# Folded weight loaded and split in the last turns, a new fixed order, and other places for chunk 6's copies

## The chip, the cores and the metric

One core of one Trainium2 chip runs the kernel. The metric is device time in microseconds of one execution, the median of several runs. TensorE (PE) does the matrix products, VectorE (DVE), ScalarE (ACT) and GpSimd (POOL) the elementwise work, and SyncE (SP) issues the transfers.

## What is computed

```python
def reference(**kwargs):            # attention, then two MLPs
    attn_out = _attn_ref(q, k, v)   # 4 x 8 heads, 576 positions, 64 wide; window masks
    x = attn_out.transpose(0, 2, 1, 3).reshape(2304, 512)
    x = _moe_ref(x, w_in, w_out)
    return _moe2_ref(x, w1, w2, w3, w_out)

def _moe_ref(x, w_in, w_out):       # 512 -> 2048 -> 512
    h = x @ w_in
    g = np.maximum(0.01 * h, h)
    return g @ w_out

def _moe2_ref(x, w1, w2, w3, w_out):   # 512 -> 1024 -> 512
    a = x @ w1
    b = x @ w2
    h = a * b @ w3
    return h @ w_out
```

Everything is float32, some of the inputs arrive as 64-bit words that the kernel converts.

## The kernel before

A float32 product is made of three matmuls on a high and a low part of each operand (`mm3`, lines 132 to 134). The two parts come from `split_steps`: a cast to the high part (L122) and a subtraction for the low one (L124), each on an engine named by the caller. So a third of TensorE's matmuls stand on each of the lines 132, 133 and 134, whatever they compute; tiles tell them apart.

The program has two halves. The first is written out by hand: the string `START` has one letter for each step of each stage, `LOADS` one letter for each load (a letter `L` in `START` takes the next one), and the instructions stand in each engine's queue in that order. It holds the attention (`ps_s`, `ps_p`, `ps_o`), the first MLP, the fold of `w3 @ w_out` of the second MLP into one weight, and the preparation of the second MLP's weights.

- The first MLP works on 7 chunks of tokens. For a chunk there are 16 turns, 112 in all: a turn makes `ps_h` (12 matmuls), its activation `g` (L545), the two parts `gs` of `g`, and adds 12 matmuls of 384 columns to the chunk's sums `ps_x`. At the end of a chunk `evacuate_steps` copies `ps_x` into `st` (L621) and stores it.
- The fold writes the product of `w3` and the last weight to memory (`wp_dram`); `w3` is transposed on TensorE (`ps_w3T`) after its conversion (`wf`).
- The weights of the second MLP are combined into seven sums per block (`weight_sums`, tiles `sum` and `ws`), and parts of the result y of the first MLP into seven sums (`sum_y_steps`: `ysum`, `ys`).

The second half is left to the scheduler. For each of 3 pairs of token chunks (p) and 8 blocks (i), `gate` makes seven products of six matmuls each into tiles `ps_m`: products 0 and 1 share a pair of banks, 2 and 3 another pair, both from two buffers called "acc"; 4, 5 and 6 have a bank each. ScalarE copies three of them (`e1`, `e2`, `e5`, L783), VectorE adds them up (`c21`, `c11`, `c22`, L787), and the gated result is split into `p` on ScalarE and GpSimd. The accumulators `ps_x` of the chunks use the two "acc" buffers too, so that the first gate must wait until they have been copied. Behind the eight gates of a p, `final` multiplies `p` by the folded weight (`ps_y`).

The folded weight is fetched in the gates of p = 0: `load_wp` loads 128 of its 1024 rows into a staging tile `wpf` (two buffers), and `split_wp` splits them on ScalarE and GpSimd into `wps`, a tile that takes over the place of an eighth of the first MLP's `w_out` (tag "wo"). Chunk 6's copies `st` take a tile of the tag "o", which has two places, where the four copies of a chunk need four.

Who splits what is set by letters in tables: A is ScalarE, D is VectorE, G is GpSimd.

Of the kernel before, what the change touches and what calls it, by code (L numbers as in the profile page):

```python
# [28 lines left out]
def tile_window_attention_two_mlps(  # L29
# [801 lines left out]
    with ExitStack():  # L831
# [71 lines left out]
        START = (
            "L~L~~~~LTL~Y~~LT~Y~~SLTMXSYLqTMXLE~~~Y~wqEwSRNTMLRPXNCSYLqEwPMTCLLXVYRqVx~NyxTEySYwL"
            "RLTMNLXPLY~CqEwSGDPMLVALRXCSNLxBL~MqEwPUVyGSLXxLARq~y~C~M~NEXVBDGwPqEwLx~R~~GN~y~C~R"
            "DANPVCDIBPUxOVLCy~IxVUAHOxGyyBIAGHLUgBODILcHgUAlIOcDgJlBOGLUcHDAlIGFBHgLAUcBHOglLIDL"
            "HGgOAUGHDgIAGDBJOALUBDGIJLUBLOILUcHAGOIlBJOALGgcBDlHZAGgUzHcADlBDUJgBDUIJcOIlGIJUcgO"
            "AIJDBlcGOJlAcDGUHBlDIOLAJULgOBIHUGOIDGAHOcBDLGAUJglBIgDJLcOAlGcUHBZLAIDzHOgBUGIcHlgA"
            "OlBGJDgLAUDBUJFLJULcLIclLISOISMlHGOMXAFqEwJGXLBOHgRAGNcBDHlqEwUDPUgJIRDgNCIcOHAlGOBD"
            "GHALUgLFAVIgJOxLBycDLBUHlIUOIJcgGlAOJBDGcULAlHIDcOBlGHgUADIHBOgULJgIO|FPJCcLlSclSMHX"  # L910
            "MqEwFVHXLgxqyJgRENwRPcFJCNlPZcHClzVgFVxLJyxyJclLLJcLlSSMXHMqEwXJqgRcHENwlPgRHcCNlPgJ"
            "CVclVxyJxGyADHBULHIOgclJgGHcADlBHgULIOHgSgSMGXJADqMBHEXLUqEwwIOHZRzNJcRlgGPJCcNADlBJ"
            "cglLUPcIOHClHgGADHgBULJIOJclgGJcADlBJclLUJcIOlHGHgDAclBHgULIOJgVclLVxHyGxyADJBgULJcF"
            "IOlJLclHLHgclHgHgFHgLSSMJFXLJcqMXlEJcqwgRlEJcNwRlFHNHgZLczlHgFJgLHclPgHCFSSMLJMXXqEw"
            "PcJlFCJqEwcLRlNJgcRlJcNFVlVxLHyxyJgclPHCSgclSMXHMqXPgEHqCwERVgNwVxLJRxyNyPclJCLSclSM"
            "FJMLFHXJgLXqcqEPwHlCRENwVgcVRxlyHxLNyFPgHCLPgJCFVVxcJLxylLyHclHgHgSSMXHMqEwXqJRENJwc"
            "RlJcNgPZlHCczlgSgSMFHXLMqJXFEJqwLcRElwPNgHCRcNlVFgVxJLxyyPcHClFSgSMJXMqEwXqPcHCRlEwN"
            "VgRNVxHyxLyPHCSSMJXMqXqEPcJCwlERgwNVRVcxNHyxlygPJCPcHClgVV^LLLLLLLprprprxJ0yxy01d1dJ"
            "c2l2L3gLJ3cl4cH5l601dWg2Wp3Lr4pL405Jr1dL5626WLc3lWp0rWpd1Lr42LW50L31Jd62p3LWrpLr4WL5"
            "061dHe2f3LpHgrpcLrJglLWclWp4rp40JL5r106L5d16W2d32LHp3LrHLgclWgWpr4LWp05r1HdL623L4gW0"  # L920
            "p5dr1W6pL2rH3LLef4J50p61dr2WcLlLJ3pgrLWicjlkWpmr4J50Lp61dr2HcLlL3WgWpr4pLW05r16LH2d3"
            "L4gW0p5dr1W6pL2rHeL3f4W50p61dWrpL2rW3L4W56JprpL4cWr5l6LWgHprpWrW!JeLLfLJcLlgJcalboJc"
            "hlLnHaHgobclhJgnL78Jc9$la%bHo&h*nLJg+ac-blH=oh<nLHg7ac8lb9Jgoh$nLJca%lb&Hho*nL+Jg-c="
            "lH<a78oHg9bclhHgnL$a%Jogb&*hJ+cLnlHc-l=Hg<a78obJ9gh$nJLca%lbHihocj&LHgn*k+mlH-g=<Ha7"
            "obJ8h9n$LJca%ob&Jhcl*LnglJcg+l-Hc=l<Hg7a8ob9H$h%gnLJ&a*ob+Jch-lL=Jcgnl<Hca7l8bo9Hgh$"
            "nHg%a&boJ*h+nHc-l=gJ<789J$c%l&Jgc*l+Jc-l=H<@sHgtclvJgssJctlvtJvssJ#tvtivjksmtvstv"
        )
# [174 lines left out]
```

## Time and profile before

| what | us |
|---|---|
| median of 3 runs | 842.15 (841.25 to 842.74) |
| the profiled execution | 842.99 |
| its span, first to last instruction | 840.8 |
| TensorE's matmuls busy | 823.4 |
| VectorE, ScalarE, GpSimd busy | 507.6, 378.8, 221.2 |

The span is measured by the profiler from the first to the last instruction of the core; 2.2 us of the execution's own time lie around it. Busy time is the time in which an engine has an instruction in work, added up over the span. TensorE's granted clock is at its higher level from 20 us on. The rest of the profile is read below in single rows.

### The profile page before, as it was taken

What the parts mean: (1) busy time and instruction counts of PE and PEld (TensorE: products, weight loads), DVE (VectorE), ACT (ScalarE), POOL (GpSimd) and SP (SyncE); (2) the same over time, 40 slices, a digit from 0 to 9 for tenths busy, and PEclk for the clock granted to TensorE, in tenths of its full rate; (3) what the DMA queues carried; (4) which work ended last, traced back from release to release, by engine and by line L of the source; (5) the groups of instructions that cost most, each with busy time, mean ns of one, the idle gap of its engine ahead of it and who ended that gap; (6) DMA issues with size and microseconds to landing.
All of it is one profiled execution on the core that took longest, in us unless ns stands there. A gap on an engine that the chain in (4) does not pass through costs nothing.

```text
span 840.8 us, 15523 instructions
## 1 busy us (share of the span) xinstructions
PE 823.4 (98%) x5818; PEld 780.1 (93%) x5818; DVE 507.6 (60%) x1001; ACT 378.8 (45%) x831; POOL 221.2 (26%) x252
## 2 busy tenths in 40 slices
PE   7999999999999999999999999989999999999998
PEld 7899999999999999899889999979988999889987
DVE  3999986444647364565545667776792277606730
ACT  3999873442233333556545665443341234213311
POOL 3514422343334334321203200025211022102210
PEclk9999999999999999999999999999999999999999
DMA  6996855445454432465638787668755377426001
GB/s 134 266 322 185 240 151 160 119 138 146 120 148 112 96 93 84 147 206 174 224 114 276 267 277 245 238 218 313 240 189 205 101 262 239 132 69 225 14 26 51
DMA packets 104570, 146.37 MB, mean 174 GB/s; under 512 B 44720, under 2 KB 70064, under 8 KB 104496
## 3 DMA queue, kind: packets, MB, share of 16 engines
q1 hardware_dynamic: 104496, 145.39, 56.2%
q8 instruction: 46, 0.75, 0.4%
q14 instruction: 28, 0.23, 0.1%
HBM read 115.87 MB, written 29.49 MB: 173 GB/s over the span
## 4 chain that ended last, share of the span: by engine, by line
PE 85%; DVE 5%; ACT 3%; DMA 3%; issue 2%; POOL 1%; SPq 0%; ACTq 0%; DVEq 0%; POOLq 0%
PE ps_h L132 7%; PE ps_x L132 7%; PE ps_h L134 7%; PE ps_x L133 7%; PE ps_h L133 7%; PE ps_x L134 7%; PE ps_m L132 7%; PE ps_m L134 7%; PE ps_m L133 7%; PE ps_y L132 4%; PE ps_y L133 4%; PE ps_y L134 4%; PE ps_s L408 3%; PE ps_o L494 2%; PE ps_p L473 2%
## 5 line engine op out<-in xcount | busy, mean ns | idle before, releaser
L132 PE MATMUL ps_h<-x,win 128*128 128x384 f32 (+2 forms) x448 | 143.0, 319 | 0.7 <-DVE win L124 0.7
L134 PE MATMUL ps_h<-x,win 128*128 128x384 f32 (+2 forms) x448 | 140.0, 312 | 0.0
L133 PE MATMUL ps_h<-x,win 128*128 128x384 f32 (+2 forms) x448 | 139.9, 312 | 0.0
L132 PE MATMUL ps_m<-ys,ws 128*128 128x384 f32 x336 | 114.1, 341 | 6.7 <-ACT e L783 6.0
L132 PE MATMUL ps_x<-gs,wout 128*128 128x384 f32 (+2 forms) x356 | 114.7, 322 | 0.2 <-ACT st L621 0.2
L133 PE MATMUL ps_m<-ys,ws 128*128 128x384 f32 x336 | 113.3, 337 | 0.0
L134 PE MATMUL ps_x<-gs,wout 128*128 128x384 f32 (+2 forms) x356 | 112.4, 316 | 0.0
L133 PE MATMUL ps_x<-gs,wout 128*128 128x384 f32 (+2 forms) x356 | 112.4, 316 | 0.0
L134 PE MATMUL ps_m<-ys,ws 128*128 128x384 f32 x336 | 111.2, 337 | 0.0
L124 POOL TENSOR_TENSOR gs<-g,gs 128x384 fp32r<-128x384 f32 (+2 forms) x70 | 65.9, 944 | 151.7 <-DVE gs L122 136.0
L124 POOL TENSOR_TENSOR p<-c,p 128x384 fp32r<-128x384 f32 x48 | 49.4, 1048 | 190.7 <-ACT p L122 185.5
L545 ACT ACTIVATE g<-ps_h 128x384 f32<-128x384 f32 (+2 forms) x112 | 49.3, 441 | 102.0 <-PE ps_h L134 73.9
L132 PEld LDWEIGHTS ps_h<-x,win 128*128 128x128 f32 x448 | 84.5, 189 | 3.0 <-issue 0.9
L133 PEld LDWEIGHTS ps_h<-x,win 128*128 128x128 f32 x448 | 84.6, 189 | 0.3
L134 PEld LDWEIGHTS ps_h<-x,win 128*128 128x128 f32 x448 | 84.5, 189 | 0.0
L787 DVE TENSOR_TENSOR c<-c,ps_m 128x384 f32<-128x384 f32 x96 | 49.7, 549 | 52.4 <-PE ps_m L134 40.6
L132 PEld LDWEIGHTS ps_m<-ys,ws 128*128 128x128 f32 x336 | 63.0, 188 | 10.6 <-ACT e L783 8.8
L783 ACT COPY e<-ps_m 128x384 f32<-128x384 f32 x72 | 34.1, 480 | 77.3 <-PE ps_m L134 46.6
L132 PEld LDWEIGHTS ps_x<-gs,wout 128*128 128x128 f32 x356 | 67.1, 189 | 1.8 <-ACT st L621 0.5
L122 DVE CAST gs<-g 128x384 fp32r<-128x384 f32 (+2 forms) x84 | 32.0, 383 | 60.2 <-PE ps_x L134 44.1
L133 PEld LDWEIGHTS ps_x<-gs,wout 128*128 128x128 f32 x356 | 67.2, 189 | 0.2
L134 PEld LDWEIGHTS ps_x<-gs,wout 128*128 128x128 f32 x356 | 67.1, 189 | 0.0
(131 smaller groups left out, 1731.0 us busy)
## 6 DMA issues: line engine op xcount, KB each, us to landing
ws<-ws_dram SPq DMA_DIRECT2D x63, 512.0 KB
raw<-in_moe_w_out_dram SPq DMA_DIRECT2D x24, 512.0 KB
ws_dram<-ws SPq DMA_DIRECT2D x24, 512.0 KB
raw<-in_moe_w_in_dram SPq DMA_DIRECT2D x16, 512.0 KB
rawf<-in_moe_w_dram SPq DMA_DIRECT2D x16, 512.0 KB
wo2f<-wo_dram SPq DMA_DIRECT2D x32, 256.0 KB
rawl<-in_moe_w_dram SPq DMA_DIRECT2D x16, 512.0 KB
q<-in_q_dram SPq DMA_DIRECT2D x48, 140.0 KB
```

The lines of the kernel that those rows point to most:

```text
L122: copy_on(e_hi)(hi, src)
L124: e_lo.tensor_tensor(lo, src, hi.bitcast(F32), op=ALU.subtract)
L132: nc.tensor.matmul(ps, a[1], b[0], start=first, stop=False)
L133: nc.tensor.matmul(ps, a[0], b[1], start=False, stop=False)
L134: nc.tensor.matmul(ps, a[0], b[0], start=False, stop=last)
L408: nc.tensor.matmul(ps[j * QB : (j + 1) * QB, i - bl.start], qt[d, i * QB : (i + 1) * QB], kt[d, first_key(i, plain) : first_key(i, plain) ...
L473: nc.tensor.transpose(pss[g][:, i - i0], s[:, i], ident)
L494: nc.tensor.matmul(ps[j * D : (j + 1) * D, i * QB : (i + 1) * QB], vt[i][:, h + j, :], t[:, i, j * QB : (j + 1) * QB], start=True, stop=True,)
L545: nc.scalar.activation(g, ps, AF.Prelu, alpha=SLOPE)
L783: nc.scalar.copy(t, a)
L787: e.tensor_tensor(t, a, b, op=op)
```

## The change

The edits:

1. The folded weight is loaded and split within the last 12 turns of `START`. `LOADS` has eight new letters `t`, `START` eight pairs `,` and `;`, for a new stage `split_wp`. The load goes straight into the low half of the place in `wo`, there is no staging tile, and the subtraction is done on VectorE in place. Each load waits for chunk 6's last matmul on the eighth of `w_out` whose place it takes.
2. Chunk 6's four copies go into two tiles of the tag "p", which has sixteen places (the results' own).
3. `e5`, `c21` and `c11` have two buffers each in the gates, like `e1` and `e2` before.
4. `START`, `LOADS` and the tables that name engines are other ones. Of the tables, in counts: the high part of the 16 turns' `gs` in the later chunks (entry `1`) goes from VectorE to ScalarE; 14 heads, not 18, take their exponentials in one instruction.

```diff
     GS_ON = {
-        0: "DG", 1: "DD",
+        0: "DG", 1: "AD",
...
                         if c == NCH - 1:
-                            st = fin.tile([P, DM], F32, tag="o", name=f"st{c}_{i}_{j}", bufs=2)[:, :n]
+                            if j == 0:
+                                st6 = fin.tile([P, 2, MT], F32, tag="p", name=f"st{c}_{i}", bufs=2 * NI)
+                            st = st6[:, j]
...
     def load_wp(ib):
-        t = fin.tile([P, DM], F32, tag="wpf", name=f"wpf{ib}", bufs=2)
-        nc.sync.dma_start(t, wp_dram[ib * P : (ib + 1) * P, :])
-        wsum[ib] = t
+        wp[ib] = wo_slot(f"wps{ib}")
+        nc.sync.dma_start(wp[ib][:, 1].bitcast(F32), wp_dram[ib * P : (ib + 1) * P, :])
 
     def split_wp(ib):
-        t = wo_slot(f"wps{ib}")
-        split(t[:, 0], t[:, 1], wsum.pop(ib), nc.scalar, nc.gpsimd)
-        wp[ib] = t
+        t = wp[ib]
+        yield from split_steps(t[:, 0], t[:, 1], t[:, 1].bitcast(F32), nc.scalar, nc.vector)
...
-        TWICE = ("e1", "e2")
+        TWICE = ("e1", "e2", "e5", "c21", "c11")
...
-            "lH<a78oHg9bclhHgnL$a%Jogb&*hJ+cLnlHc-l=Hg<a78obJ9gh$nJLca%lbHihocj&LHgn*k+mlH-g=<Ha7"
+            "ohH$nLm%aJ&bo*h+JLcnL-lJcLgl=g<HcL7al8ob9H$h%gnLJ,&a;*obJL+,-c;hJLl=Lng,<cHL;alc7blH"
...
+            ",;": split_wp,
...
+                    elif y == "t":
+                        load_wp(len(wp))
...
                 gate(p, i)
-                if p == 0:
-                    load_wp(i)
-                    split_wp(i)
```

How the change moves instructions is shown at three places. In the names below, the number behind the last underscore is a serial number of the tile.

*ScalarE's queue at the passage from the last turn into the gates.* Before, with the copies `st6`, the casts of `wps` and the copies `e10_0` and `e20_0` of the first gate:

```order
551 L621 COPY st6_0_1_6691<-ps_x6_0_0_6180 128x384
552 L122 CAST wps0_6793<-wpf0_6791 128x512
553 L783 COPY e10_0_6720<-ps_m0_0_0_6719 128x384
554 L122 CAST wps1_6878<-wpf1_6876 128x512
555 L621 COPY st6_1_1_6699<-ps_x6_0_1_6181 128x384
556 L783 COPY e20_0_6728<-ps_m0_0_0_6719 128x384
557 L122 CAST ys0_5_6702<-ysum0_5_6697 128x768
558 L122 CAST wps2_6967<-wpf2_6965 128x512
559 L122 CAST wps3_7052<-wpf3_7050 128x512
560 L783 COPY e10_1_6805<-ps_m0_1_0_6804 128x384
561 L783 COPY e50_0_6755<-ps_m0_0_2_6736 128x384
```

The same place in the changed kernel:

```order
575 L122 CAST ys0_4_6722<-yf0_5596 128x768
576 L122 CAST ys0_5_6727<-ysum0_5_6724 128x768
577 L623 COPY st6_0_6729<-ps_x6_0_0_6199 128x384
578 L623 COPY st6_1_6735<-ps_x6_0_1_6200 128x384
579 L783 COPY e10_0_6755<-ps_m0_0_0_6754 128x384
580 L122 CAST ys0_6_6742<-ysum0_6_6738 128x768
581 L783 COPY e20_0_6763<-ps_m0_0_0_6754 128x384
582 L783 COPY e50_0_6790<-ps_m0_0_2_6771 128x384
583 L783 COPY e10_1_6835<-ps_m0_1_0_6834 128x384
584 L783 COPY e20_1_6843<-ps_m0_1_0_6834 128x384
```

The casts of `wps` are gone from between the copies, and the cast of `ys0_5` stands ahead of the copies `st6`.

*TensorE's queue in gate 4 of p = 0.* Before, with the end of the second product (`ps_m0_4_0` from `ys0_1`) and the beginning of the third (`ps_m0_4_2`):

```order
3230 L132 MATMUL ps_m0_4_0_7063<-ys0_1_6642,ws0_4_1_6798 128x384
3231 L133 MATMUL ps_m0_4_0_7063<-ys0_1_6642,ws0_4_1_6798 128x384
3232 L134 MATMUL ps_m0_4_0_7063<-ys0_1_6642,ws0_4_1_6798 128x384
3233 L132 MATMUL ps_m0_4_2_7080<-ys0_2_6646,ws0_4_2_6800 128x384
3234 L133 MATMUL ps_m0_4_2_7080<-ys0_2_6646,ws0_4_2_6800 128x384
```

In the changed kernel the third product of that gate stands ahead of the second, which follows here:

```order
3239 L134 MATMUL ps_m0_4_2_7095<-ys0_3_6688,ws0_4_1_6828 128x384
3240 L132 MATMUL ps_m0_4_4_7117<-ys0_4_6722,ws0_4_2_6830 128x384
...
3249 L132 MATMUL ps_m0_5_6_7215<-ys0_6_6742,ws0_5_3_6916 128x384
3250 L132 MATMUL ps_m0_4_0_7078<-ys0_1_6651,ws0_4_1_6828 128x384
3251 L133 MATMUL ps_m0_4_0_7078<-ys0_1_6651,ws0_4_1_6828 128x384
3252 L134 MATMUL ps_m0_4_0_7078<-ys0_1_6651,ws0_4_1_6828 128x384
```

Where the third product followed the second at once, ten matmuls of other products and the second one now stand behind the third.

*ScalarE's queue in chunk 6, from the activation of `ps_h6_8` to that of `ps_h6_9`.* Before (`lw` and `rl` are the conversion of weights):

```order
519 L545 ACTIVATE g_85<-ps_h6_8_6285 128x384
520 L117 ACTIVATE lw12_6301<-rawl13_6242 128x512
521 L122 CAST ws0_0_2_6348<-sum0_2_6344 128x2x256
522 L163 ACTIVATE rl13_6346<-rawl13_6242 128x512
523 L165 ACTIVATE rl13_6346<-rawl13_6242 128x512
524 L122 CAST ws0_0_3_6373<-sum0_3_6368 128x2x256
525 L545 ACTIVATE g_85<-ps_h6_9_6310 128x384
```

In the changed kernel, the first twelve of what stands there:

```order
534 L545 ACTIVATE g_85<-ps_h6_8_6293 128x384
535 L122 CAST wps2_6279<-wps2_6279 128x512
536 L122 CAST gs_1825<-g_85 128x384
537 L117 ACTIVATE lw14_6400<-rawl14_6313 128x512
538 L122 CAST gs_1825<-g_85 128x384
539 L163 ACTIVATE rl14_6401<-rawl14_6313 128x512
540 L122 CAST ws0_1_0_6423<-sum1_0_6405 128x256
541 L165 ACTIVATE rl14_6401<-rawl14_6313 128x512
542 L122 CAST ws0_1_1_6428<-lw12_6283 128x2x256
543 L122 CAST wps3_6349<-wps3_6349 128x512
544 L117 ACTIVATE lw14_6400<-rawl15_6376 128x512
545 L122 CAST wps4_6371<-wps4_6371 128x512
```

Three more follow (two `rl`, one `ws`) before the `g` of `ps_h6_9`: three casts of `wps`, two of `gs` and a second conversion have come in between the two activations.

## Rows read from the trace of the kernel before

**Rows 1.** The page: busy time by engine, and the chain that ended last.

```profile
PE 823.4 (98%) x5818; PEld 780.1 (93%) x5818; DVE 507.6 (60%) x1001; ACT 378.8 (45%) x831; POOL 221.2 (26%) x252
...
PE 85%; DVE 5%; ACT 3%; DMA 3%; issue 2%; POOL 1%; SPq 0%; ACTq 0%; DVEq 0%; POOLq 0%
```

**Rows 2.** TensorE's waits, 552 us to the end, then before: total, times, longest.

```profile
PE ps_m L132 <- ACT e L783: 6.0, 8, 1.4
PE ps_m L132 <- ACT st L621: 0.7, 2, 0.4
...
PE ps_w3T L665 <- DVE wf L169: 0.8, 1, 0.8
...
PE ps_h L132 <- DVE win L124: 0.7, 1, 0.7
```

**Rows 3.** Timeline of TensorE: start, duration, instruction, in brackets the idle time before.

```profile
554.50 0.34 PE L134 MATMUL ps_m<-ys,ws 128*128 128x384 f32 x1
555.95 0.44 PE L132 MATMUL ps_m<-ys,ws 128*128 128x384 f32 x1 [1.12 <-ACT e L783]
556.23 0.34 PE L133 MATMUL ps_m<-ys,ws 128*128 128x384 f32 x1
...
613.53 0.45 PE L132 MATMUL ps_m<-ys,ws 128*128 128x384 f32 x1 [0.62 <-ACT e L783]
```

**Rows 4.** Timeline of ScalarE at the passage.

```profile
554.90 0.62 ACT L122 CAST wps<-wpf 128x512 fp32r<-128x512 f32 x1 [2.32 <-DMA wpf<-wp_dram]
555.42 0.47 ACT L783 COPY e<-ps_m 128x384 f32<-128x384 f32 x1
```

**Rows 5.** The chain that ended last, 552 to 564 us: start, duration, what.

```profile
552.99 3.30 DMA x_dram<-st
...
558.36 4.06 DMA wpf<-wp_dram
...
562.45 0.62 ACT wps L122
```

**Rows 6.** VectorE: one row of its timeline, and of its waits from 552 to 640 us.

```profile
556.41 0.56 DVE L621 COPY st<-ps_x 128x384 f32<-128x384 f32 x1 [3.72 <-DMA x_dram<-st]
...
DVE c L787 <- POOL p L124: 9.6, 12, 1.3
```

**Rows 7.** A stretch of the windows: length, busy time (instructions) by engine, clock, DMA.

```profile
640.00:660.00 20.00, 20.00 (x92) 16.82 (x91) 0.56 (x1) 2.28 (x4) 1.01 (x1) 1.00 0.27 85
```

**Rows 8.** The instructions on the tile `wpf`: duration in ns, least, median, most.

```profile
L122 ACT CAST wps<-wpf x8: 617/620/627, 554.9 to 579.6; 128x512 fp32r<-128x512 f32 x8
L124 POOL TENSOR_TENSOR wps<-wpf,wps x8: 1281/1285/1296, 555.6 to 582.1; 128x512 fp32r<-128x512 f32 x8
```

**Rows 9.** VectorE by form, 477 to 640 us: busy, mean ns, idle time before.

```profile
L124 DVE TENSOR_TENSOR gs<-g,gs 128x384 fp32r<-128x384 f32 x16 | 8.9, 554 | 0.1
L124 DVE TENSOR_TENSOR ws<-sum,ws 128x512 fp32r<-128x512 f32 x12 | 8.3, 690 | 4.5 <-ACT ws L122 4.5
...
L122 DVE CAST gs<-g 128x384 fp32r<-128x384 f32 x17 | 6.1, 359 | 7.2 <-PE ps_x L134 4.5 <-ACT g L545 1.5 <-POOL gs L124 0.9
...
L748 DVE TENSOR_TENSOR ysum<-yf 128x768 f32<-128x768 f32 x4 | 3.8, 953 | 0.0
```

**Rows 10.** The sum of five windows of 15 us, 477 to 552 us (chunk 6).

```profile
sum 75.00, PE 75.00 PEld 74.92 DVE 54.35 ACT 42.20 POOL 1.73; mean PE 15.00 PEld 14.98 DVE 10.87 ACT 8.44 POOL 0.35
```

**Rows 11.** Timeline of TensorE at the first transposed block of `w3`.

```profile
346.95 0.34 PE L134 MATMUL ps_x<-gs,wout 128*128 128x384 f32 x1
348.10 0.66 PE L665 MATMUL ps_w3T<-ident,wf 128*128 128x128 f32 x4 [0.81 <-DVE wf L169]
```

**Rows 12.** The sum of five windows of 20 us, 20 to 120 us.

```profile
sum 100.00, PE 98.06 PEld 93.17 DVE 93.31 ACT 90.26 POOL 38.47; mean PE 19.61 PEld 18.63 DVE 18.66 ACT 18.05 POOL 7.69
```

**Rows 13.** The instructions on the tile `yf`, 555 to 580 us: ns, first and last start.

```profile
L748 DVE TENSOR_TENSOR ysum<-yf,yf x3: 1397/1603/2054, 556.9 to 572.5; 128x768 f32<-128x768 f32 x3
L741 SPq DMA_DIRECT2D yf<-x_dram x2: 371/433/495, 563.3 to 563.7; - x2
```

More of the change, by code (lines that the diff above doesn't have):

```diff
@@ L177, in tile_window_attention_two_mlps @@
     FOLD_CONV = ("GAD",)
-    P_ON = "ADDAAAAAAAAADDADAAAAAAAAAAAAAAAA"
-    X_ON = "AADADADDADADDADDAAAAAAAAAAAAAAAA"
-    ONE_EXP = (0, 3, 6, 11, 13, 14, 16, 17, 20, 21, 22, 23, 25, 26, 27, 29, 30, 31)
+    P_ON = "ADDAAAAADAADDDAAAAAAAAAAAAAAAAAA"
+    X_ON = "AADADADDADADDAAAAAAAAAAAAAAAAAAA"
+    ONE_EXP = (0, 1, 3, 6, 11, 13, 16, 17, 19, 20, 27, 28, 29, 31)
     GS_ON = {
[7 rows of a table removed]
[7 rows of a table added]
     }
-    TURN_ON = "ADAADAAA"
+    TURN_ON = "AAAADDAA"
     MLP_CONV = (
-        "GDG DAG GDD DAD AAD DAD AAD DDD DAD AAD DAD DAD GAG GAD GAD GAD "
-        "AAD AAD ADD GDD GAD ADG GAG DAD AAD GDD DAG AAD GAD DAD GAD DDD "
+        "GDG DAG DDD DAD AAD DAD AAD DDD DAD AAD DDG DAD DAG DAD GAD GAD "
+        "AAD AAD AAD DDD GAG AAG GAG DDD AAD ADD GAD DAD DAD AAD AAD GAD "
         "GAD GAD GAD GAD GAD GAD GAD GAD"
@@ L697, in tile_window_attention_two_mlps @@
     ws_dram = tc.dram_tile([NI, P, NM * 4 * P], F32, name="ws_dram")
-    ws, wsum, words_of = {}, {}, {}
+    ws, words_of = {}, {}
     PLACE = ((0, 0), (1, 0), (2, 0), (1, 1), (2, 1), (3, 0), (3, 1))
@@ L870, in tile_window_attention_two_mlps @@
         }
-        RAW_AT = "WWWWWWWWWWWWWWWWNWWNWWNWWWNWWNWNNNNNNNNN"
-        PAIR_AT = "VVKKVVVKVVKKVVKKVWKVKKVKKVKKWKKKVVVVVVVV"
+        RAW_AT = "WWWWWWWWWWWWWWWWNWWWNWNWWWNWWNWNNNNNNNNN"
+        PAIR_AT = "VVKKVVVKVVKKVVKKVWKVKKVKKVKKVKWKVVVVVVVV"
         def raw_early(i):
@@ L903, in tile_window_attention_two_mlps @@
         START = (
[L904 to L923, printed above, removed]
@@ L924, in tile_window_attention_two_mlps @@
-            "lH<a78oHg9bclhHgnL$a%Jogb&*hJ+cLnlHc-l=Hg<a78obJ9gh$nJLca%lbHihocj&LHgn*k+mlH-g=<Ha7"
-            "obJ8h9n$LJca%ob&Jhcl*LnglJcg+l-Hc=l<Hg7a8ob9H$h%gnLJ&a*ob+Jch-lL=Jcgnl<Hca7l8bo9Hgh$"
-            "nHg%a&boJ*h+nHc-l=gJ<789J$c%l&Jgc*l+Jc-l=H<@sHgtclvJgssJctlvtJvssJ#tvtivjksmtvstv"
+            "L~L~~~~LTL~Y~~LT~Y~~SLTMXSYLqTMXLE~~q~Y~wESRNwTMLRPXNCSYLqEwPMTCLXLVYqVx~RxTyENySYwL"
+            "RLTMNLXPLY~CLqEwSGDPMVALRXCSNLxBL~MqEwPUVyGSLXCLRq~AM~DxVNXEy~BwPqEwGL~R~D~N~x~C~GRA"
+            "DPNyVCIBUPOxVLCy~IxVUGHOyAxyBDIHAGLOgBUAcHLUIlgOIcDJBOGlLUgAHDGIFAHcglBOcHLUBlgLIDHG"
@@ new lines, in tile_window_attention_two_mlps @@
+            "LgOAUGHDgIAGOBHDALUBGJDILUBOILJUcLAOlBGJgcGLAlIBDOHZgAczUHBlDIGgUJAOIDGBJDcOAJcBlUGl"
+            "HIcDlAOgJBDUgLGUJLIcUAlIHOBDLcOIUJgGOIlJcAGlBOHALDGBDUAJDIUBOHgILGZcUzlHAOIDBGJgUAOg"
+            "cJIDlcBGOALHBlUGFJgLAcBDLlSILUSLOMHXDqEwIMHFgcXHGLlLgDAOqEwJRGUNAJIRDBNcOBPUJgLGcIAU"
+            "OBHDIGCAHgOBlcDlGPUgHAlIDUBJOILUgGOJCcGADlIBVDOAHcLUxBlyIJUgOILO|JcFHlLSgcSMlJXMqEwX"
+            "VFHqxLREyNHgwcRlPgNJCFLPZHczlCHgFVgVxLJxLyyJclFJLclSLSMXHMqEwXJqgRcHENwlPgRHcNClPgJC"
@@ new lines, in tile_window_attention_two_mlps @@
+            "VclVxyJxGyADHBULJIOgclHGHgDAclBHgULIOJgHZczlSgGSMADHXMBXqEwLUHIOgRqEwNHRGPJANCDBPcUL"
+            "JClIOgJclVcgGVxHAlyxDBGyULHADIOgBHULIOJLJclgGJcADlBJcglLUHcIOlHgHgGJADBJULcFIOJlLcgl"
+            "HcLlJgHclFJgLSclSMHMXFHgqXLHgqEwHERwNJRNFJcLlJcglJgcFlLHZczlHgPgJFCLHclHgSSMJFXLJcqE"
+            "wMlXPFHCqgLRJEcNwlJcRglNVcVxlJyxyPclHCSgSMXHMqXPgEHCwqEwRHNVgRNVxLHyxyPJCLSclSMgFJXL"
+            "MJqEwcFPlXLJCcRlqEwNJcglRJcNlVFVxHxLyLyPgJCclPFHCLVgcVxlJyxLyHHgclHgSgSMXHMqEwXHRqEw"
@@ new lines, in tile_window_attention_two_mlps @@
+            "NPRJCNSclSMFJgMHLZczFPJlCXLXqEwqVcgRlEVxwHLNxygRyNFJPcJClFgJclSclSMHMXXqPgqHECwERwNV"
+            "gVxRJyxLNyPcHlCPgHCSSMHXMqEwXqVREVNxJwxyRyNPcJlCgPcJClgVclV^LLLLLLLprprprxJyx0y01d1d"
+            "Jc2l2L3LH3Hgcl4gJ0561d2Wc3LlWpr4pLH05r16L2d4gW0L5316Wpd2rWp3LLr4LW5061dJ23LWclpr4pJ0"
+            "L5r1dL62W3LHepfrp4Wg0L5r1dLH62c3LlWgpWrpLr4W50L61dH23Lp4grWp0L5r1H6L2d3LJprJcLlgWclW"
+            "prWpLr4eLH50f61d2Wp3LgrJpLrL4iH50jc6l1k2dWg3LmWpr4pLJ05r16L2dWc3LlWpr4pW0L5r16HL2d3L"
@@ new lines, in tile_window_attention_two_mlps @@
+            "WgprWpLr4H50eL6fd142W0p31dWrp2LrJ53L64cW5l6pWgrpLrHL4W56pWrprWW!JeLLfLJcLlgJcalboJch"
+            "lLnHaHgobclhJgnL78Jc9$la%bHo&h*nLHg+ac-blJ=og<hnJLca7l8boH9$h%JnLgc&laH*ob+h-JgnL=c<"
+            "Hla7boHghcl8L9$Jng%a&bJco*lh+HLn-=Jg<c7alH8ob9hH$nLg%a&cHgo*lb+Jg-h=nLH<cia7jl8Hkg9b"
+            "ohH$nLm%aJ&bo*h+JLcnL-lJcLgl=g<HcL7al8ob9H$h%gnLJ,&a;*obJL+,-c;hJLl=Lng,<cHL;alc7blH"
+            "o8h9$n,J%a;,&bJL;*oh+gJnL,-cg;=Hlc<,l7,H;8g;9$cH%gl&J*g+-Jc=l<@JscltHvssJgctlHvtvJgs"
@@ L927, in tile_window_attention_two_mlps @@
+            "scltJvJ#tsvtivjksmtv"
         )
         LOADS = (
-            "0123a45b67wcwwwdwww8wwwwwwwwwwwwwwwwew9wAwwwwBwwwfCDEFgwwhwwwwwwGiHIjJKLMNOPklQR"
-            "oSTpUVmnyyzzzzzyyyzzyzzyyzzyzzzzyyzzzyzyzzyzzzyzzyzzzzzzxrxsxxxxxxxxxxxxxx"
+            "0123a45b67wcwwwwdww8wwwwwwwwwwwwwwwwwew9AwwwwwwwBfCDEFwghwwwwwwwiGHIjJKLMNOPklQR"
+            "oSTpUVmnyyzzzzzyyyzzyyzzyzzyzzyzzyzzyzzzyzzyzzyzzyzzzzzzxrxsxxxxxxxxxxxtxttxttxt"
+            "tt"
         )
```

12 rows, old and new, of the table GS_ON are left out of this document.

## The prediction, made before the changed kernel ran

> **What bounds the kernel now.** I read the share of busy time first: TensorE's matmuls fill 823.4 of 840.8 us and hold 85% of the chain that ended last [rows 1]. So a change can gain only where TensorE stands still. The list of what it waited for comes next [rows 2]. In the gate stage (552 us to the end) eight waits for the copies `e` take 6.0 us and two for the copies `st` take 0.7 us. Before 552 us the largest waits past the start-up are 0.8 us of `ps_w3T` for `wf` and 0.7 us of `ps_h` for `win`.
>
> A wait costs more than its gap. At 555.95 us the gap is 1.12 us, yet from the matmul at 554.50 to the one at 556.23 there are 1.73 us where two pitches of 0.175 would be 0.35: 1.38 us lost. So each wait loses its gap plus some 0.27 us; the gap of 0.62 at 613.53, the most frequent, loses 0.90 [rows 3]. The ten waits of the gate stage lose 6.7 + 10 x 0.27 = 9.4 us. They come in two kinds.
>
> *The passage into the gates.* Losses by that rule: 0.66 us (552.64), 1.39 (555.95), 0.58 (557.58) and 1.70 (563.50), together 4.33 us. The gap at 555.95 has its reason on ScalarE's queue: the cast of `wps` at 554.90 first waited 2.32 us for its load, and the copy `e` behind it came at 555.42 [rows 4]. The one at 563.50 is read from the chain: the third copy of chunk 6 needed a place that the store of an earlier copy held for 3.30 us, the load of a `wpf` behind it landed after 4.06 us, then came the cast of 0.62 us, then the copy `e`, then TensorE [rows 5]. VectorE shows the same from its side: 3.72 us idle until that store [rows 6], and then the longest `ysum`, 2.05 us [rows 13].
>
> *A pair of products behind its own copy.* At 582.25, 590.50, 613.53 and 707.09 us, and a little later in the pair at 625.47 and 719.03, the product that comes next writes into the pair of banks that the copy of the product just finished must still empty. That is 4 x 0.90 + 0.74 + 0.75 = 5.09 us.
>
> The Trainium skill ("Perfetto Trace Analysis", Identifying the Most-Contended Engine) says that matmul busy time is no measure of headroom and that the share of weight loads is one. By it the room would be what the 780.1 us of loads leave, 60.7 us. The trace disagrees here: from 640 to 660 us TensorE is busy 20.00 of 20 us while the loads show 16.82, because 512-column matmuls outlast their loads [rows 7]. The sum below uses the waits.
>
> **The change, part by part.**
>
> *Folded weight.* Eight loads of 256 KB, eight casts of 0.62 us on ScalarE and eight subtractions of 1.28 us on GpSimd [rows 8] leave the first gates. In the last turns of START there are then eight loads, eight casts of 0.62 us and eight subtractions on VectorE, which takes 0.69 us for that shape [rows 9]. In chunk 6's 75 us TensorE has no gap at all: 75.00 busy of 75, with VectorE at 54.35 and ScalarE at 42.20 [rows 10]. The same chunk now also has the high part of 14 `gs` on ScalarE (the copy `e` of that size took 0.47 us, [rows 4]) and not on VectorE (0.36 us, [rows 9]). ScalarE goes to 42.2 + 5.0 + 6.6 = 53.8 us, VectorE to 54.4 + 5.5 - 5.0 = 54.9. Both fit in 75 on average, so I price this at 0; what it costs without that cover is the third rival.
>
> *Chunk 6's copies.* Their tiles come from the sixteen places of the results, not from two, so the 3.30 us store holds up no copy. No wait is added: those places are free until the first `p`.
>
> *Passage.* After the change no `wps` stands in ScalarE's queue between the copies, and one cast and two subtractions fewer of the y sums are left after the last turn. Before: 4.33 us. What is left is bounded below by half of the smallest loss there (0.3) and above by one two-term `ysum` coming late (1.4 us at the least, [rows 13]; 1.5). VectorE has some 11.7 us of work from the first `ysum` to the second copy `st6` (two two-term sums of 1.4, seven other sums or subtractions of 0.95, three `gs` and a copy of 0.55, [rows 9]), and TensorE six blocks of twelve matmuls, 12.5 us, above it. I take 1.0: a gain of 3.3 us (2.8 to 4.0).
>
> The skill ("SBUF — State Buffer", Who interferes with whom) says that a VectorE instruction with two SBUF inputs and a GpSimd instruction that reads SBUF shut each other out for a whole instruction. The `ysum` of 2.05 us beside a `wps` on GpSimd agrees (the shortest took 1.4). By the rule the passage would be at its lower end, 0.3, and the time 0.7 us lower.
>
> *Second places for e5, c21, c11, and a new order of the gates.* VectorE no longer waits for GpSimd's `p` before it writes the next c21 (9.6 us in twelve waits from 552 to 640, [rows 6]), the copy e5 no longer waits for the last use of e5, and the banks come free earlier. I went through the order for every `ps_m` matmul whose copy follows at most five matmuls behind the work that it copies. Before there are six in the gates proper, those of the 5.09 us. In the changed one there are three: the second product of gate 3 directly behind its own copy (0.90), and those of gates 5 and 7 four matmuls behind (0 each at best, 0.75 at worst, as the pairs three behind). I take 1.5 (0.9 to 2.4): a gain of 3.6 us (2.7 to 4.2).
>
> *The wait for `wf` at 348.10 us* [rows 11]. Between the last `ps_o` and that `ps_w3T` stand 48 matmuls where there were 36: 8.3 us of cover, not 6.2, for work that came 0.81 us too late. The loss of 0.98 us (1.15 from start to start less a pitch) goes but for some hundredths: a gain of 0.9 us (0 to 0.9).
>
> *The start (20 to 120 us)*, with its own new order: VectorE is busy 93.31 of 100 us and ScalarE 90.26 [rows 12], so that what is moved between them shows at once. VectorE gets 0.9 to 1.6 us more before the first `ps_h` and ScalarE 0.9 less; against that the wait of 0.7 us for `win` and one of 0.3 for GpSimd's `s` have more matmuls ahead of them. I take 0 (1.2 either way). The rest of the moves, four exponentials by row not by head among them, lie at 120 to 440 us, where the list has no wait over 0.3 us but that for `wf`: 0.
>
> *Sum.* 3.3 + 3.6 + 0.9 = 7.8 us. The profiled execution took 842.99 us (2.2 outside the span), 0.84 above the median of the runs. 842.99 - 7.8 = 835.2, and less 0.84 is 834.4 us. The bounds of the four terms, not all at one end, make 832.3 to 837.0 for this case.
>
> **The rivals.**
>
> 1. *More is gained (13%).* The start's two waits also go (1.0 + 0.6 with what each loses behind its gap), no gate waits but gate 3 and the passage is fed: 834.4 - 1.6 - 0.6 - 0.7 = 831.5 us. For it: fewer short distances. Against: the start's two engines are nearly full.
>
> 2. *Part is given back at the edges (18%).* The loads of `yf2` and `yf3` are read one gate earlier on VectorE: they took 8.8 us from issue (563.7) to the sum that waited for them (572.5) [rows 13], and VectorE now reaches them about 8.8 us after the last turn; TensorE needs what is queued behind only some 9 us later. With a start 1.2 us later and two gates at 0.75 us, or with a load late by 12 us, 2 to 5 us come back: 836.4 to 839.4.
>
> 3. *ScalarE stands at the new casts, and the kernel gets slower (6%).* The casts of `wps` now stand ahead of activations `g` that TensorE's next `ps_h` need, and each can start only when its load has landed, which can be issued only when the last turn's matmul on that place is done. From `ps_h6_7` to `ps_h6_14` there are 192 matmuls, 33.2 us. At the rate of before ScalarE works 42.2 / 75 of that, 18.7 us; with eight casts of `wps` (5.0) and eight of `gs` (3.8) it is 27.5. So some 6 us of waiting are free, and each one more moves TensorE. The tightest piece is between the `g` of `ps_h6_8` and that of `ps_h6_9`, with fourteen instructions where there were five. Before, the first cast waited 2.32 us [rows 4]. The change gains nothing from 6 + 7.8 = 13.8 us of waiting (1.7 a cast), and is 0.2% slower from 15.5; with 2.3 us at each of the eight, 18.4 us, the time is 834.4 + 12.4 = 846.8. Against it: the loads stand several instructions ahead of their casts.
>
> 4. *No net change (4%)*: rival 3 at 12.5 to 15.5 us of waiting, 841 to 843.9.
>
> **How the numbers follow.** The forecast holds 59%. 832.3 to 837.0 is its own range. For 8 in 10 I leave out the lower half of rival 1, a small part of rival 2 and rivals 3 and 4, and go to 831.5 and 839.5. Faster by over 0.2% (1.7 us, about what a measurement of this kernel can tell from none) has 59 + 13 + 18 = 90%; within it 4%; slower 6%.
>
> **What would show it.** Right: the list of waits of `ps_m` for `e` falls from eight and 6.0 us to one to three and under 2; no wait for `st` at the passage; the 12 last turns still without a gap; `ps_w3T`'s wait under 0.2 us. Wrong: gaps of `ps_h` or `ps_x` for `g` or `gs` from 500 to 550 us behind a cast of `wps` that waited for its load; a gap of `ps_m` for VectorE 10 to 20 us after the last turn behind `ysum`; a first `ps_h` more than 1.5 us later than at 40.6 us.

## The result, and the profile after

| | us |
|---|---|
| before, 4 runs beside the changed kernel | 842.44 (841.25 to 842.86) |
| changed, 4 runs | 834.17 (833.46 to 834.42) |
| ratio | 0.9904 (0.9889 to 0.9918) |
| the profiled execution of the changed kernel | 833.46, span 831.7 |

Faster by 8.3 us, 0.2 us from the forecast of 834.4. Two more sets of runs of the same changed kernel (below) gave 834.45 and 834.22.

The page of the changed kernel, busy time and chain, answers to [rows 1]:

```profile
PE 820.4 (99%) x5816; PEld 779.3 (94%) x5816; DVE 501.1 (60%) x991; ACT 389.6 (47%) x881; POOL 209.5 (25%) x236
...
PE 86%; DVE 4%; ACT 3%; SPq 3%; DMA 2%; issue 1%; POOL 0%; ACTq 0%; DVEq 0%; POOLq 0%
```

ScalarE has 10.8 us more work and GpSimd 11.7 us less, as the folded weight's subtractions left GpSimd and the high parts of `gs` came to ScalarE.

TensorE's waits in the changed kernel, from 552 us to the end (two rows), then from 12 to 552 us (four), each with total, times and longest:

```profile
PE ps_m L132 <- DVE c L787: 0.8, 2, 0.4
PE ps_m L132 <- ACT e L783: 0.6, 1, 0.6
...
PE ps_h L132 <- ACT g L545: 1.0, 1, 1.0
PE ps_s L408 <- ACT kT L392: 0.8, 1, 0.8
PE ps_s L408 <- DVE kT L318: 0.6, 1, 0.6
PE ps_s L408 <- DVE x L520: 0.4, 1, 0.4
```

Against [rows 2]: the eight waits for `e` are one, both for `st` are gone, and so are those for `wf` and `win`. New are two waits of `ps_m` for VectorE's `c`, and in the start one for `g` and one for `kT`.

Stretches of 20 us of the changed kernel: length, busy time of PE, PEld, DVE, ACT and POOL, granted clock, share of the DMA engines, GB/s:

```profile
540.00:560.00 20.00, 20.00 (x117) 20.00 (x116) 13.26 (x20) 9.12 (x16) 0.00 (x0) 1.00 0.57 184
560.00:580.00 20.00, 19.38 (x110) 18.89 (x109) 14.56 (x29) 6.50 (x15) 5.92 (x6) 1.00 0.82 281
580.00:600.00 20.00, 19.60 (x112) 19.27 (x111) 13.11 (x27) 6.33 (x14) 4.68 (x6) 1.00 0.76 258
600.00:620.00 20.00, 19.60 (x105) 18.37 (x104) 16.18 (x26) 7.48 (x13) 3.93 (x4) 1.00 0.64 199
```

TensorE was busy 18.18, 18.57, 18.75 and 19.38 us in these stretches of the kernel before, of which the first was:

```profile
540.00:560.00 20.00, 18.18 (x102) 17.22 (x101) 12.49 (x17) 8.55 (x14) 2.52 (x2) 1.00 0.63 198
```

The passage into the gates, at 549.93, now lies in a full stretch. TensorE's timeline there has no gap at all where [rows 3] had one of 1.12 us:

```profile
549.76 0.33 PE L134 MATMUL ps_x<-gs,wout 128*128 128x384 f32 x1
549.93 0.51 PE L132 MATMUL ps_m<-ys,ws 128*128 128x384 f32 x2
550.28 0.33 PE L133 MATMUL ps_m<-ys,ws 128*128 128x384 f32 x1
```

Where the 9.5 us between the two profiled executions came from is read from marks in the two timelines. The last `ps_o` began at 340.6 and now begins at 339.7, with one matmul fewer ahead of it: 0.9 us up to there, for which the granted clock of the execution before is the reason (below, at the start). The first `ps_w3T` moved from 348.1 to 348.3 with 12 more matmuls ahead of it (2.1 us): 1.9 us up to there, so 1.0 us between the two marks, the wait for `wf`. To the first `ps_m` another 0.1 us. From there to the end of the span 288.9 us became 281.8: 7.1 us in the passage and the gates. 0.4 us more lies outside the span.

### The profile page after: what moved, and what is told of

It is laid out like the page before. It is cut to its first block, busy times and chain, and to the rows that moved or that the text cites. A ratio compares the mean times of both kernels' runs of the same rounds, so it can differ in the third digit from the quotient of the medians.

```text
span 831.7 us, 15497 instructions
## 1 busy us (share of the span) xinstructions
PE 820.4 (99%) x5816; PEld 779.3 (94%) x5816; DVE 501.1 (60%) x991; ACT 389.6 (47%) x881; POOL 209.5 (25%) x236
## 4 chain that ended last, share of the span: by engine, by line
PE 86%; DVE 4%; ACT 3%; SPq 3%; DMA 2%; issue 1%; POOL 0%; ACTq 0%; DVEq 0%; POOLq 0%
PE ps_x L132 7%; PE ps_m L132 7%; PE ps_h L132 7%; PE ps_x L134 7%; PE ps_x L133 7%; PE ps_m L134 7%; PE ps_m L133 7%; PE ps_h L134 7%; PE ps_h L133 7%; PE ps_y L132 4%; PE ps_y L133 4%; PE ps_y L134 4%; PE ps_s L408 2%; PE ps_o L494 2%; PE ps_wp L134 2%; PE ps_wp L133 2%
## 5 line engine op out<-in xcount | busy, mean ns | idle before, releaser
L122 DVE CAST gs<-g 128x384 fp32r<-128x384 f32 (+2 forms) x70 | 24.5, 350 | 65.1 <-PE ps_x L134 54.3
```

The costliest lines, as they stand in the source:

```text
L122: copy_on(e_hi)(hi, src)
```

## The experiments

The theory of the prediction says that the second places of `e5`, `c21` and `c11` free the pairs of banks (3.6 us), and that the loads of the folded weight, taken out of the first gates, free the passage (3.3 us). Its rivals: (a) the pairs wait only because of the order in which the scheduler puts the three products of a gate, and any edit that makes it choose another order is enough; (b) it does not matter where `START` has the new letters, only that the load goes into a place that is free early; (c) the copies' new tiles (edit 2) count, or do not. Edit 3 by itself was not tried: while the staging tiles `wpf` are there, the second places find no room.

**Edit 2 alone**, on the kernel before:

```diff
-                            st = fin.tile([P, DM], F32, tag="o", name=f"st{c}_{i}_{j}", bufs=2)[:, :n]
+                            if j == 0:
+                                st6 = fin.tile([P, 2, MT], F32, tag="p", name=f"st{c}_{i}", bufs=2 * NI)
+                            st = st6[:, j]
```

> The kernel before with edit 2 alone (chunk 6's copies in the results' places). Theory A (what a gate waits for is decided by the order that the scheduler gives the products, and any edit near the gates changes that order): in this kernel no product follows its own pair's copy within seven matmuls, so the 5.1 us of those six waits go although no gate tile has a second place; the passage keeps about 4 us, since a cast of wps still stands ahead of the second copy st6. About 837.3 us, list of waits of ps_m for e under 3.5 us. Rival B (the six waits go only where e5, c21 and c11 have second places): only what the store's 3.30 us cost at 563.5 goes, at most 1.7 us: 840.7 to 842.4, with six waits of 0.5 to 0.6 us left.

Measured: 837.95 us (835.36 to 840.54), ratio 0.9951 (0.9935 to 0.9968). TensorE's waits from 500 us to the end, of the run of 835.36:

```profile
PE ps_m L132 <- ACT st L623: 1.4, 2, 1.0
PE ps_m L133 <- DVE ys L124: 0.7, 1, 0.7
PE ps_m L132 <- ACT e L785: 0.4, 1, 0.4
PE ps_m L132 <- DVE c L789: 0.2, 1, 0.2
```

What is left lies in the passage (551 to 561 us), but for the 0.2 us for `c` in gate 4. The waits for `e` of the pairs are gone without one second place.

**Edit 1 alone**, on the kernel before: load in place, subtraction on VectorE, the new letters set into the old `START` (shown here) and `LOADS`, everything else as it was.

```diff
...
-            "obJ8h9n$LJca%ob&Jhcl*LnglJcg+l-Hc=l<Hg7a8ob9H$h%gnLJ&a*ob+Jch-lL=Jcgnl<Hca7l8bo9Hgh$"
-            "nHg%a&boJ*h+nHc-l=gJ<789J$c%l&Jgc*l+Jc-l=H<@sHgtclvJgssJctlvtJvssJ#tvtivjksmtvstv"
+            "obJL8h9n$LJLca%ob&JL,hcl*LnglJL,;cg+l-Hc=l<Hg7a8ob9H$h%gnLJL,;&a*ob+JL,;ch-lL=JL,;cg"
+            "nl<Hca7l8bo9Hgh$nHg%a&boJL,;*h+nHc-l=gJ,;<789J,;$c%l&J;gc*l+Jc-l=H<@sHgtclvJgssJctlv"
+            "tJvssJ#tvtivjksmtvstv"
...
```

> The kernel before with edit 1 alone: eight loads and eight splits of the folded weight put into the last turns of its own old order, each load behind chunk 6's turn whose place it takes, each cast two turns later; tables, copies and buffers as before. Theory A: no product stands close behind its pair's copy here either (minus 5.1 us), the casts are gone from the passage but the third copy of chunk 6 still waits for a store of 3.30 us, so some 2.4 of 4.3 us are left there (minus 1.9): about 835.4 us, and no gap of TensorE from 500 to 550 us. Rival B: the six waits stay, 840.5. Rival C (ScalarE or the loads are too slow in the last turns): gaps of ps_h or ps_x from 500 to 550 us, over 838.

Measured: 835.48 us (834.91 to 836.73), ratio 0.9923 (0.9911 to 0.9935). Its waits from 500 us on:

```profile
PE ps_m L132 <- DVE c L785: 1.0, 2, 0.6
PE ps_m L132 <- ACT st L621: 0.4, 1, 0.4
```

One of the four edits gives 6.5 us of the 8.3, with the copies in two places and with the old second places. Three casts of `wps` waited 3.8 us for their loads on ScalarE, and TensorE had no gap from 500 to 550 us: the room that rival 3 of the prediction speaks of is real.

**Edits 1, 2 and 3**, with the order and the tables of before (the two diffs above and `TWICE` as in the change).

> The kernel before with edits 1, 2 and 3, with its old order and tables. Theory A: the passage loses under 1 us (minus 3.5), three waits in the gates are left, one of 0.9 and two of 0.2 to 0.7 us (minus 3.2): about 835.7 us; the changed kernel's further 1.5 us are the wait for wf at 348 us, one for st at 408 us and the start. Rival D (the new order and tables bring most of the gain): 839 or more.

Measured: 837.39 us (836.01 to 840.0), ratio 0.9945 (0.9929 to 0.996). This is not faster than edit 1 alone, which was expected otherwise. So the other two edits are worth nothing in the old order, and the new order and tables (edit 4) some 3 us beside them (837.39 to 834.17). From 500 us on its waits come to 3.9 us: two for `c` (1.2 and 0.4), one of 1.0 for `st`, one of 0.7 for `g` and one of 0.6 for `e`; the waits for `wf` and `win` of [rows 2] are still there.

**The folded weight written in the gates again**, in the changed kernel: still in place, with the low part on GpSimd, and without the letters `t`, `,` and `;`.

```diff
...
                 gate(p, i)
+                if p == 0:
+                    load_wp(i)
+                    run(split_wp(i))
```

> The changed kernel with the loads and splits of the folded weight written in the gates of p = 0 again, but straight into their places (no staging tiles), with the subtraction on GpSimd. Theory E: what matters is that the load needs no tile of the pool that opens only after the last turn; the scheduler then moves loads and casts up into the last turns by itself, so the time is that of the changed kernel, 834.2 within 0.8 us, with the casts of wps from 505 to 530 us. Rival F: written in the gates they come as late as before, and the passage loses some 3 us: 837.

Measured: 833.84 us (833.12 to 835.34), ratio 0.9903 (0.989 to 0.9917): as the changed kernel. The scheduler drew the eight loads forward by itself, and the casts stand from 508.9 to 528.8 us. Rival (b) holds as far as `START` goes: where it has the letters does not matter. That the place, free before the first gate, is what lets the scheduler do so is read from the kernel; no run has the old staging tiles in an early place.

**The changed kernel again**, beside the next three.

> The changed kernel once more, unchanged, as the measure for the other three on the same chip: 834.2 within 0.8 us by every theory.

Measured: 834.45 us (833.24 to 835.65). In the run of 835.65 there was one stall more, at 568.96, behind a `ysum` that waited 2.0 us for its `yf`. VectorE's waits of the first changed execution, 552 to 640 us, had the same one, shorter:

```profile
DVE c L787 <- ACT e L783: 17.4, 8, 4.8
DVE ysum L750 <- DMA yf<-x_dram: 2.8, 2, 1.4
```

The wait for GpSimd's `p` of [rows 6] is gone from this list. The new wait for `yf` is that of rival 2 of the prediction; TensorE feels it in some runs, as here by a gap of 0.48 us.

**One second place at a time**, in the changed kernel:

```diff
-        TWICE = ("e1", "e2", "e5", "c21", "c11")
+        TWICE = ("e1", "e2", "c11")
```

> The changed kernel with a second place for c11 alone, none for e5 and c21. Theory A (the order that the scheduler makes of the gates decides, not the number of places): in this order no product follows its pair's copy within seven matmuls, nor VectorE's release within sixteen, so the changed kernel's three waits in the gates (0.90, 0.67 and 0.67 us lost) go: 832.0 us, no wait of ps_m in the list. Rival B (places are what matters): fewer places bring waits back, 834.2 to 838.

Measured: 835.03 us (832.31 to 836.43), ratio 0.9909 (0.9892 to 0.9927). The median misses the 832.0 and lies in the range of rival B, so that the time alone does not speak for the order. The six runs fall apart by the mean granted clock that each one lists: 1.000 and 0.999 in those of 832.93 and 832.31, 0.995 to 0.998 in the four of 834.90 to 836.43. A mean of 0.996 over 834 us is 6.7 us at half the clock, in which 3.3 us of work are lost (an estimate), about what lies between the two groups. The six runs of edit 2 alone do the same: 0.999 and 1.000 in the three fastest (835.36 to 837.52), 0.996 to 0.998 in the three slowest (838.38 to 840.54). In the profiled run of 832.31 no wait for `e` was left, with a place less for `e5` and `c21`, but one of 1.0 us for `c`, which the expectation did not have.

```diff
-        TWICE = ("e1", "e2", "e5", "c21", "c11")
+        TWICE = ("e1", "e2", "c22")
```

> The changed kernel with a second place for c22 alone, none for e5, c21 and c11. Theory A: in this order six products of p = 0 stand none or one matmul behind their pair's copy and six more of p = 1 none or three: 6 x 0.75 to 0.9 and 6 x 0.9 us lost where the changed kernel loses 2.2, so 834.2 - 2.2 + 10 = 842 us, with a list of eleven or twelve waits of ps_m for e. Rival B: one place fewer than in the changed kernel costs at most what before lost in its pairs: 834.2 to 837.

Measured: 844.79 us (842.73 to 846.38), ratio 1.003 (1.0019 to 1.0042), slower than the kernel before. Its waits from 500 us on:

```profile
PE ps_m L132 <- ACT e L783: 7.5, 11, 2.2
PE ps_m L132 <- DVE c L787: 0.7, 1, 0.7
PE ps_y L132 <- DVE c L787: 0.4, 1, 0.4
```

One second place more than the kernel before, its loads and tiles as in the change, and the waits for `e` are back, eleven of them. The programs as built say why. A product has to wait for a copy `e` when it writes into the pair of banks that ScalarE has still to copy. For the second product of a gate this is always the pair of the first, since the two share a tile; for the third it depends on which of the two pairs the scheduler gave it. I counted in all 24 gates the products that stand at most three matmuls behind the product whose copy they need, and set beside them the waits of `ps_m` for `e` in the gates:

| kernel | second behind first | third behind second, in the same pair | waits for `e` |
|---|---|---|---|
| before | 0 | 6 | 6 (and two in the passage) |
| edit 2 alone | 0 | 0 | 0 (and one in the passage) |
| edit 1 alone | 0 | 0 | 0 |
| edits 1, 2, 3 | 1 (gate 4) | 0 | 1 |
| changed | 1 (gate 3) | 0 | 1 |
| `c11` only | 0 | 0 | 0 |
| `c22` only | 7 | 5 | 11 |

With `c22` only it is the second product that waits in six gates of p = 0, and the third in five of p = 1. To stand close behind is not enough: in gates 5 and 6 of p = 0 of the kernel before the third product follows the second at once, but in the other pair, and TensorE does not wait. Rival (a) holds: the number of second places does not go with the waits; the order does, with the pairs of banks that come with it.

**ScalarE's free room**: each `wps` is cast three times in the changed kernel, 16 casts of 0.62 us more, 9.9 us in chunk 6.

```diff
         t = wp[ib]
+        for _ in range(2):
+            nc.scalar.copy(t[:, 0], t[:, 1].bitcast(F32))
```

> The changed kernel with each cast of wps done three times: 16 more casts of 0.62 us, 9.9 us of ScalarE, between the turns where the eight stand. Nothing else of the result changes. The prediction's third rival counted some 6 us of ScalarE free there and every further one on TensorE's path: 834.2 + 3 to 4 = 837.5 to 838.5 us, with gaps of ps_h for g from 508 to 530 us. If ScalarE's queue has far more room than that, nothing: under 835. If a cast more is on the path at once: 844.

Measured: 840.54 us (839.27 to 842.05), ratio 0.9983 (0.9973 to 0.9993), 6.1 us above the changed kernel beside it, 2 to 3 more than expected. TensorE's timeline has two gaps for `g`, and behind the first one matmuls 0.32 us apart, not 0.175:

```profile
527.21 0.45 PE L132 MATMUL ps_h<-x,win 128*128 128x384 f32 x1 [1.91 <-ACT g L545]
...
529.10 0.53 PE L133 MATMUL ps_h<-x,win 128*128 128x384 f32 x1
529.42 0.53 PE L134 MATMUL ps_h<-x,win 128*128 128x384 f32 x1
...
535.08 0.44 PE L132 MATMUL ps_h<-x,win 128*128 128x384 f32 x1 [1.87 <-ACT g L545]
```

Stretches of 2 us there (columns as above, the granted clock third from the end):

```profile
527.00:529.00 2.00, 1.79 (x7) 1.80 (x8) 1.15 (x3) 1.94 (x5) 0.00 (x0) 0.71 0.67 242
529.00:531.00 2.00, 2.00 (x7) 2.00 (x7) 1.86 (x4) 2.00 (x5) 0.00 (x0) 0.50 0.50 152
531.00:533.00 2.00, 2.00 (x12) 1.89 (x11) 1.25 (x3) 1.94 (x4) 0.00 (x0) 0.94 0.60 240
```

The two gaps with some 0.27 us behind each are 4.3 us, some ten matmuls at half the clock 1.5 us: 5.8 of the 6.1. So of 9.9 us more on ScalarE 4.3 reached TensorE and 5.6 were free; the prediction had "some 6 us". The fall of the clock is what the expectation lacked.

**The two-term `ysum` of later pairs on GpSimd** (k = 0, p of 1 and 2), against the wait for `yf` on VectorE:

```diff
-            nc.vector.tensor_tensor(s, *terms, op=TERMS[k][2])
+            (nc.gpsimd if p and k == 0 else nc.vector).tensor_tensor(s, *terms, op=TERMS[k][2])
```

It was run beside the changed kernel for the third time, and with `TWICE` as before.

> The changed kernel a third time, as the measure for the two beside it: 834.3 within 0.8 us; in the gates three waits from 575 to 612 us (0.90, 0.67, 0.67 us lost) and one at some 569 us of 0 to 0.7.

Measured: 834.22 us (833.27 to 834.41).

> The changed kernel with the first sum of y of the later pairs (ysum1_0, ysum2_0) on GpSimd, so that VectorE does not stand at the load of yf2 and yf3 in gate 0; all second places kept. Theory A (order): the scheduler's order of the gates is another one again, with no product within seven matmuls of its pair's copy: the three waits and the one behind ysum go, 834.3 - 2.2 - 0.3 = 831.8 us, no wait of ps_m over 0.2 us from 555 to 640. Rival: GpSimd's sum, over 1.9 us long and waiting for the load, holds up the parts p behind it, and c21 and c11 with them: 834 to 836.

Measured: **831.21 us** (830.44 to 831.37), ratio 0.9865 (0.985 to 0.988): faster than both kernels. From 500 us to the end the list of TensorE's waits is empty. GpSimd takes the wait over; of its waits from 552 to 640 us:

```profile
POOL ysum L750 <- DMA yf<-x_dram: 11.2, 1, 11.2
```

The scheduler's order changed with it: in gates 3, 5 and 7 twelve matmuls lie between the first and the second product where the changed kernel has 0, 4 and 4. So the 3.0 us are the three stalls of the gates and the wait for `yf` together; the run does not part the two.

> As the kernel with that sum on GpSimd, but without edit 3: e5, c21 and c11 have one place each, as before. Theory A: here too the order has no product close behind its pair's copy, so it is as fast as the one with second places, 831.8 to 832.5. Rival B (second places are what took the waits away): VectorE waits for GpSimd's p and the pair waits are back, six of 0.9 us: 836 to 838.

Measured: 833.61 us (832.22 to 834.14), ratio 0.9892 (0.9873 to 0.9911), between its two theories. No wait for `e` came, but one of 1.2 us for `c`, at 568.77. VectorE's timeline ahead of it:

```profile
566.09 0.55 DVE L787 TENSOR_TENSOR c<-e,ps_m 128x384 f32<-128x384 f32 x1 [0.91 <-POOL p L124]
567.06 0.56 DVE L787 TENSOR_TENSOR c<-e,ps_m 128x384 f32<-128x384 f32 x1 [0.41 <-POOL p L124]
568.16 0.55 DVE L787 TENSOR_TENSOR c<-c,ps_m 128x384 f32<-128x384 f32 x1 [0.55 <-ACT e L783]
```

With one place for `c21` VectorE waits for GpSimd's `p`, as in [rows 6], and TensorE feels it once: 1.2 us and the 0.27 behind the gap. So the second places are worth some 1.5 us, with the 2.4 us between the two kernels as the upper end. The run does not part them wholly from the order: in gates 2, 4 and 6 it has twelve matmuls between the first and the second product where the kernel with the second places has eighteen.

**Edit 2 taken back** in that faster kernel: the copies in the two places of the tag "o".

> The kernel with the first sum of y on GpSimd and all second places (831.2), with edit 2 alone undone: chunk 6's copies in the two places of the tag o again. If the passage needs edit 2, its third copy stands for the store of 3.30 us that held it before, and TensorE loses 1.7 us or more some 4 us after the last turn: 833 or more. If the store took so long only because loads of the folded weight were queued with it, the copy waits 1 to 1.5 us as in the run with edit 1 alone and TensorE loses 0 to 0.6: 831.2 to 831.8.

Measured: 831.57 us (830.88 to 832.54), ratio 0.9866 (0.9844 to 0.9887): no difference that the runs can tell. The third copy waits for a place again, on VectorE's timeline:

```profile
551.92 0.56 DVE L621 COPY st<-ps_x 128x384 f32<-128x384 f32 x1 [1.16 <-DMA x_dram<-st]
```

It waits 1.16 us where it was 3.72 in [rows 6], and TensorE has no gap. With edit 1 alone, which keeps the two places too, it was 1.15 us. In both runs the loads of `wpf` no longer stand in the queue with the stores, which is the likely reason.

## Why the prediction was right, and where it was not

**What bounds the kernel: right.** The time went where TensorE's waits went, not with the busy time of another engine. The Trainium skill ("Perfetto Trace Analysis", Identifying the Most-Contended Engine) would see 52.4 us of room left in the changed kernel, 831.7 of span less 779.3 of weight loads. The trace of the faster kernel disagrees again: no wait is left in it after 500 us, at a span of 829.6.

**The passage: the mechanism was right, the term too small.** 3.3 us (2.8 to 4.0) were forecast with 1.0 left; nothing was left, a gain of 4.3 us. VectorE was the engine in doubt. Its two-term `ysum` took 0.94 to 0.96 us in the changed kernel, not the 1.4 to 2.05 of [rows 13]:

```profile
L750 DVE TENSOR_TENSOR ysum<-yf,yf x9: 942/957/959, 535.2 to 715.9; 128x768 f32<-128x768 f32 x9
```

The Trainium skill ("SBUF — State Buffer", Who interferes with whom) has VectorE with two SBUF inputs and GpSimd exclude each other. The trace agrees: GpSimd was idle from 540 to 560 us (0.00 busy, above), and of the nine such sums of the kernel before the five that took 1.31 to 2.05 us lay beside an instruction of GpSimd, the four that lay beside none took 0.95 to 0.96. The prediction gave 0.3 us left by that rule and took 1.0 all the same; the rule was the nearer. Of the two edits meant for the passage only the first counted: edit 1 alone left 0.7 us of it (the wait of 0.4 for `st` and what is lost behind it), and edit 2 was worth nothing once edit 1 was in. Which of the things that edit 1 takes out of the passage counts most, the loads, the casts or GpSimd's subtractions, no run tells.

**The pairs: the size was near, the reason half wrong.** 3.6 us were forecast; 5.09 became 0.90 + 0.67 + 0.67 = 2.24, a gain of 2.9. Gate 3 stalled as said. The gap there and the two others of the changed kernel:

```profile
575.05 0.45 PE L132 MATMUL ps_m<-ys,ws 128*128 128x384 f32 x1 [0.62 <-ACT e L783]
590.50 0.44 PE L132 MATMUL ps_m<-ys,ws 128*128 128x384 f32 x1 [0.40 <-DVE c L787]
605.92 0.44 PE L132 MATMUL ps_m<-ys,ws 128*128 128x384 f32 x1 [0.40 <-DVE c L787]
```

The step "those of gates 5 and 7 four matmuls behind (0 each at best, 0.75 at worst)" looked at the wrong matmul. The second product of gate 5 did not wait; the third one did, for VectorE. The second product of gate 4 stands only 14 matmuls ahead of it. VectorE's timeline ahead of the stall at 590.50:

```profile
588.33 1.02 DVE L787 TENSOR_TENSOR c<-e,ps_m 128x384 f32<-128x384 f32 x2 [4.75 <-ACT e L783]
589.26 0.55 DVE L787 TENSOR_TENSOR c<-e,e 128x384 f32<-128x384 f32 x1
589.89 0.56 DVE L787 TENSOR_TENSOR c<-c,ps_m 128x384 f32<-128x384 f32 x1
```

That product's copy came late: VectorE had idled 4.75 us for it, and only behind four operations, at 590.45, are the banks that the third product needs free. TensorE has then stood for 0.40 us. And the step "Second places for e5, c21, c11, and a new order of the gates" credited the places and the order together. The runs part them: where the order keeps a product away from the copy that it needs, the waits for `e` are gone, with or without second places, and one second place that turns the order brings them back. For the waits of VectorE for `p` the places are worth some 1.5 us, 2.4 at most.

**The wait for `wf`: right**, 0.9 us forecast, 1.0 gained. The three runs with the old order of `START` kept the wait (0.7 to 0.8 us).

**The start: right, it gained nothing.** 0 (1.2 either way) was said. The mark at the last `ps_o` came 0.9 us earlier, but by the clock: the profiled execution before was at the lower level from 17.0 to 20.4 us. Its row there (the clock third from the end; the changed kernel has 1.00):

```profile
17.00:20.00 3.00, 2.97 (x21) 2.62 (x23) 1.33 (x3) 1.10 (x5) 0.82 (x1) 0.50 0.75 170
```

That is 3.4 us at half the clock, in which 1.7 us of work are lost (an estimate). The runs of edit 1 alone and of edits 1, 2 and 3 have the old start without such a fall; their last `ps_o` began at 339.5 and 339.6 us, no later than the 339.7 of the changed kernel. One set of waits took the place of another: `kT` and `g` (0.6 and 1.0) for `win` and others.

**The last turns at no cost: right.** Chunk 6 in the changed kernel, 477 to 552 us, against [rows 10]:

```profile
sum 75.00, PE 74.90 PEld 74.58 DVE 56.47 ACT 52.12 POOL 1.13; mean PE 74.90 PEld 74.58 DVE 56.47 ACT 52.12 POOL 1.13
```

ScalarE was put at 53.8 us and VectorE at 54.9. TensorE lacks 0.1 us of a full 75. Rival 3 did not come: the casts waited 0.7 us in all for their loads, where it needed 13.8 for the gain to be gone. How the loss grows beyond the free room the run with more casts shows: 9.9 us of work more cost 6.1.

**Rival 2** came in part, and was paid for by the passage. The sum was 7.8 us; by the profiles the three terms are 4.3 + 2.9 + 1.0 = 8.2. The profiled executions differ by 0.9 for the clock in the start and 0.4 outside the span beside that, 9.5 in all. By the medians it is 8.3, since the execution profiled before lay 0.55 us above its median and the one after 0.71 below. That the forecast came within 0.2 us is in part luck: the passage gave 1.0 more than was said, above its bounds, and the pairs 0.7 less.

What stays open: in which runs the clock falls, and why. The scatter of two kernels goes with it, but of the runs that were not profiled only the mean clock is known. Open is also what makes the scheduler turn the order with an edit.
